# Expert scores of the first two query tiles: whole tiles in three float32r passes instead of exchanged halves in float32

## The chip, the cores and the metric

The kernel runs on one core of a Trainium2 chip. The metric is the device time of one execution in microseconds (us). The time before is 422.52 us, the median of 3 runs (422.43 to 423.71). One more execution was recorded by the hardware profiler; all durations below are from it.

## What is computed

The reference is a sparse attention over 8 batches, 8 heads, 576 positions and head size 64, followed by a mixture of four experts (E = 4), each of which is a causal attention of its own over x, the first attention's output (8 x 576 x 512):

```python
for e in range(E):
    q = x @ wq[e]; k = x @ wk[e]; v = x @ wv[e]          # 576 x 64 each
    scores = scale * (q @ k.transpose(0, 2, 1))
    causal = np.triu(np.ones((S, S), dtype=bool), 1)
    scores = np.where(causal, -1000000000.0, scores)
    scores = scores - scores.max(-1, keepdims=True)
    a = np.exp(scores)
    a /= a.sum(-1, keepdims=True) + 1e-09
    ye = a @ v @ wo[e]
    for kk in range(K):                                   # the two chosen experts
        mask = topk[:, :, kk] == e
        out += mask[..., None] * w[:, :, kk:kk + 1] * ye
```

## The kernel before

Everything is written as small operations (`op`), each with one engine or a choice of two, and the tiles that it reads and writes. A list of numbers, ORDER, fixes the order in which all 2579 operations are issued; SECOND names those that take the second engine of their choice; FILL puts extra matmuls on the identity (L305), whose result nobody reads, ahead of some operations. Each engine works its own instructions strictly in this order.

Stage 1 (`stage1`) makes x: for each batch and each pair of heads it loads q, k and v, turns them, takes local or strided scores, a softmax, and splits x into a high and a low float32r part (`xh`, `xl`). Stage 2 works by batch and by pairs of experts (`ep` is 0 or 1; the two experts of a pair, a = 0 and 1, lie in the lower and upper 64 partitions):

- `project` makes q and k of a pair, 128 partitions by 576 columns, in two cuts of 256 and 320 columns (CUT). Each cut is 12 matmuls (L966; L977 in the first batch), four blocks of x by three products of high and low parts.
- The cuts leave PSUM so: k as float32 (`pj_out`), and from there as a high and a low float32r part (`k_h` L997, `k_l` L1001). Of q the first cut, which serves query tiles 0 and 1, stays float32 (`pj_out`); the second, for tiles 2 and 3, goes straight into high and low parts (`qk_h` L987 on ACT, `qk_l` L989 on DVE), and its last 64 columns also as float32 (`q_out`) for the 64 rows of tile 4.
- `attend` takes scores. Tiles 2 and 3 (`s2`, L1059) go in three passes, high by high, low by high and high by low, 6 matmuls of 384 or 512 columns, float32r, on the array cut as 64 rows by 128 columns. Tiles 0 and 1 (`s2q`, L1047) go in float32 on quarters of 64 by 64, in 8 matmuls: each quarter takes a half tile of 64 queries, and the two halves of tile 0 stand exchanged in PSUM, so that quarters with nearly as many columns run side by side. Such an operation is in the program once per batch and pair, 16 times in all. The recorded float32 matmuls count two to one in the program.
- Since tile 0 is exchanged, it has a mask of its own (`m_sw`, filled by `swapped` on POOL), its gate weights are copied across (`gate_s` into `wts`, 16 small copies), and its output is stored in two halves.
- Tile 4's 64 rows of two pairs are scored by `s2_4` (L1081, float32, quarters), by the cuts of 256 and 320 key columns.
- Then come mask and maximum (`max2`, L1016 on DVE), the exponential (L1021, ACT), the scaling (L1117, POOL), turning (`t2`, L1144), the product with v (`acc`, L1183), and the output projection (`out_tile`, L1217).

A matmul's operands cut the array in different ways (128x128, 64x128, 64x64, 128x64, 32x64, 64x32), and ORDER changes between these cuts 142 times.

Of the kernel before, what the change touches and what calls it, by code (L numbers as in the profile page):

```python
# [22 lines left out]
def attention_moe_kernel(  # L23
# [60 lines left out]
    class Ring:  # L84
# [36 lines left out]
    }  # L121
    ORDER = [
# [136 lines left out]
    ]  # L259
    FILL = {  # L260
        7: 1, 17: 7, 80: 4, 132: 3, 134: 3, 139: 1, 216: 2,
    }

    def op(kind, eng, key, fn, r=(), w=(), mode=None, dmas=(), after=()):
# [70 lines left out]
    def act(n):  # L335
        return 0.06 + 0.00082 * n
# [58 lines left out]
    def swapped(e):  # L395
        nc.gpsimd.memset(m_sw, 0.0)
        keep(m_sw[:64], [[-1, 128]], 64, 1)
        keep(m_sw[64:, :64], [[-1, 64]], 0, 1)
        nc.gpsimd.memset(m_sw[64:, 64:], NONE)
# [895 lines left out]
```

## Time and profile before

| | us |
|---|---|
| median of 3 runs | 422.52 |
| the profiled execution's own time | 422.69 |
| its span, first to last instruction | 421.0 |
| PE (TensorE) busy | 411.0 (98%) |
| DVE (VectorE) busy | 339.8 (81%) |
| ACT (ScalarE) busy | 277.5 (66%) |
| POOL (GpSimd) busy | 230.3 (55%) |

Busy time is the union of an engine's instructions; matmuls overlap each other, so their mean durations are longer than the distance from one to the next. What an operation takes of PE is read here from its start to the start of the next one.

### The profile page before, as it was taken

How to read it: one execution, taken by the hardware profiler on the slowest of the kernel's cores; microseconds unless marked ns; L12 is line 12 of the kernel's file. 1: busy time of each engine (PE TensorE's matmuls, PEld its weight loads, DVE VectorE, ACT ScalarE, POOL GpSimd, SP SyncE). 2: the span in 40 equal slices, each digit the busy share in tenths (PEclk: the TensorE clock that was granted, in tenths of full speed). 3: DMA queues.
4: the chain of work that ended last, by engine and by line, in shares of the span. 5: the costliest groups of instructions: out<-in, count | busy, mean ns of one | idle time of the engine just before them, and what ended most of it. 6: DMA issues, size and time to landing. Idle time of an engine off the chain costs nothing.

```text
span 421.0 us, 18647 instructions
## 1 busy us (share of the span) xinstructions
PE 411.0 (98%) x7523; PEld 358.8 (85%) x7523; DVE 339.8 (81%) x1073; ACT 277.5 (66%) x877; POOL 230.3 (55%) x398
## 2 busy tenths in 40 slices
PE   8889999999999999999999999999999999999996
PEld 5668988987898879998899888998899888997775
DVE  4897898999998899978976699898988896339840
ACT  5677378668776457877767465765666469657862
POOL 5674673776536750699229630589216671185540
PEclk9999999999999999999999999999999999999999
DMA  6667637554656655464356524750443040001033
GB/s 178 194 192 181 121 91 136 100 89 96 112 102 109 146 126 87 94 129 103 72 90 133 134 46 114 129 107 11 114 102 97 20 116 22 2 26 27 27 101 100
DMA packets 156502, 41.86 MB, mean 99 GB/s; under 512 B 146080, under 2 KB 149792, under 8 KB 156416
## 3 DMA queue, kind: packets, MB, share of 16 engines
q1 hardware_dynamic: 156272, 40.54, 43.9%
q8 instruction: 59, 0.97, 1.0%
q14 instruction: 27, 0.22, 0.2%
q10 hardware_dynamic: 144, 0.13, 0.1%
HBM read 31.20 MB, written 9.44 MB: 97 GB/s over the span
## 4 chain that ended last, share of the span: by engine, by line
PE 86%; DVE 5%; ACT 3%; DMA 2%; issue 1%; POOL 1%; SPq 0%; ACTq 0%; POOLq 0%
PE bank L966 22%; PE bank L1217 12%; PE bank L1183 10%; PE bank L895 10%; PE bank L1144 6%; PE bank L1059 5%; PE bank L783 3%; PE bank L802 3%; PE bank L1047 2%; PE bank L689 2%; PE bank L673 2%; PE bank L1081 2%; PE bank L753 2%; PE bank L977 1%; DMA p<-in_q_dram 1%
## 5 line engine op out<-in xcount | busy, mean ns | idle before, releaser
L1021 ACT ACTIVATE p<-p,st 128x384 f32<-128x384 f32 (+3 forms) x128 | 71.5, 561 | 10.8 <-DVE st L1016 10.7
L1117 POOL TENSOR_SCALAR p<-p,st,wt 128x256 f32<-128x256 f32 (+2 forms) x96 | 63.9, 672 | 15.1 <-DVE st L1108 7.4
L1016 DVE CUSTOM_DVE_ANT_0 p<-bank,m_cau 128x384 f32<-128x384 f32 (+2 forms) x96 | 50.0, 548 | 1.2 <-PE bank L1059 0.6
L1183 PE MATMUL bank<-th,vs 128*64 128x192 f32 (+4 forms) x512 | 48.0, 337 | 0.0
L563 DVE STREAM_TRANSPOSE qkt<-nat 128x576 f32<-128x576 f32 x48 | 47.5, 1002 | 0.1
L1183 PEld LDWEIGHTS bank<-th,vs 128*64 128x64 f32 x512 | 33.8, 137 | 13.8 <-issue 7.1
L345 ACT COPY th<-bank 128x256 f32<-128x256 f32 (+2 forms) x108 | 40.4, 434 | 7.6 <-PE bank L1144 7.2
L765 ACT CAST xh<-bank 128x128 fp32r<-128x128 f32 (+4 forms) x112 | 29.4, 320 | 22.3 <-PE bank L783 12.8
L966 PE MATMUL bank<-xh,wh_k 128*128 128x256 f32 (+1 forms) x120 | 36.3, 303 | 0.0
L895 PE MATMUL bank<-wh_v,xh 128*128 128x260 f32 x128 | 36.2, 283 | 0.0
L895 PE MATMUL bank<-wl_v,xh 128*128 128x260 f32 x128 | 36.2, 283 | 0.0
L966 PE MATMUL bank<-xh,wh_q 128*128 128x256 f32 (+1 forms) x120 | 36.1, 301 | 0.1
L767 DVE TENSOR_TENSOR xl<-bank,xh 128x128 fp32r<-128x128 f32 (+4 forms) x112 | 31.8, 322 | 5.3 <-ACT xh L765 5.0
L895 PE MATMUL bank<-wh_v,xl 128*128 128x260 f32 x128 | 35.9, 281 | 0.0
L966 PE MATMUL bank<-xl,wh_k 128*128 128x256 f32 (+1 forms) x120 | 35.5, 296 | 0.0
L966 PE MATMUL bank<-xh,wl_k 128*128 128x256 f32 (+1 forms) x120 | 35.5, 296 | 0.0
L966 PE MATMUL bank<-xl,wh_q 128*128 128x256 f32 (+1 forms) x120 | 35.5, 296 | 0.0
L966 PE MATMUL bank<-xh,wl_q 128*128 128x256 f32 (+1 forms) x120 | 35.5, 296 | 0.0
L1144 PEld LDWEIGHTS bank<-ident,p 64*128 64x128 f32 x800 | 30.2, 139 | 5.7 <-issue 1.3
L716 POOL TENSOR_TENSOR p1l<-p1l,st 128x640 f32<-128x640 f32 (+1 forms) x18 | 20.7, 1151 | 25.7 <-DVE st L714 25.5
L1144 PE MATMUL bank<-ident,p 64*128 64x64 f32 x800 | 33.7, 226 | 0.5 <-DVE p1l L703 0.3
L727 POOL TENSOR_TENSOR p1l<-p1l,st 128x640 f32<-128x640 f32 (+1 forms) x18 | 20.5, 1141 | 18.6 <-DVE st L725 15.2
(190 smaller groups left out, 1220.1 us busy)
## 6 DMA issues: line engine op xcount, KB each, us to landing
nat<-in_q_dram SPq DMA_DIRECT2D x96, 72.0 KB
nat<-in_k_dram SPq DMA_DIRECT2D x96, 72.0 KB
out_dram<-ys SPq DMA_DIRECT2D x23, 256.0 KB
v<-in_v_dram SPq DMA_DIRECT2D x96, 40.0 KB
out_dram<-ys SPq DMA_DIRECT2D x25, 128.0 KB
v<-in_v_dram SPq DMA_DIRECT2D x48, 54.0 KB
v<-in_v_dram SPq DMA_DIRECT2D x32, 48.0 KB
v<-in_v_dram SPq DMA_DIRECT2D x32, 45.0 KB
```

The source lines that it names most:

```text
L345: (nc.scalar.copy if e == "ACT" else nc.vector.tensor_copy)(dst, src)
L563: op("tq", {"DVE": 0.66 if local else 1.11}, k0 - 13, lambda e, x=x: nc.vector.transpose(turned(qkt.t, x), raw(x) if local else raw(x).rea ...
L765: op("xh", {"ACT": act(n_) + 0.04 * (not local)}, key, lambda e, s_=s_, x_=x_: nc.scalar.copy(x_(xh.t), s_(xa.t)), r=[xa], w=[xh[u]])
L767: op("xl", {"DVE": dve(n_)}, key + 0.5, lambda e, s_=s_, x_=x_: nc.vector.tensor_sub(x_(xl.t), s_(xa.t), x_(f(xh.t))), r=[xa, xh[u]], w=[x ...
L895: nc.tensor.matmul(vp.t[:, :NV], xx.t[:, t0:t0 + 128], ww.t[:, kt, :], start=i == 0, stop=i == 11)
L966: nc.tensor.matmul(pj.t[:, :n_], ww.t[:, kt, ep * 128:(ep + 1) * 128], xx.t[:, c], start=i == 0, stop=i == 11)
L1016: op("max2", {"DVE": 0.08 + 0.00104 * nk}, k_ + 0.5, lambda e, a=a: nc.vector.tensor_tensor_reduce(out=p.t[:, a, :nk], in0=sp[a].t[:, so:s ...
L1021: op("exp2", {"ACT": 0.285 + 0.00084 * nk}, k_ + 1, lambda e, a=a: nc.scalar.activation(p.t[:, a, :nk], p.t[:, a, :nk], AF.Exp, bias=st.t[ ...
L1117: lambda e, p=p, a=a, ci=ci, t=t, nk=nk, s_=s_, ep=ep: nc.gpsimd.tensor_scalar(p.t[:, a, :nk], p.t[:, a, :nk], s_.t[:, 20 + ci + a:21 + ci ...
L1144: nc.tensor.transpose(tp[hf].t[:, 64 * c:64 * c + 64], src, ident[r, r])
L1183: nc.tensor.matmul(acc.t[o, c0:c0 + cn], vw, th[ep, a].t[:, s0:s0 + cn], start=j == 0, stop=j == nj - 1, skip_group_check=True)
L1217: nc.tensor.matmul(yp.t[:, :n_], xx.t[:, c0:c0 + 128], ww.t[:, ep, c], start=i == 0, stop=i == 5)
```

## The change

The first cut of q is now split into high and low parts like the second; `qk_h` and `qk_l` are issued for both cuts and the float32 copy of the first cut is gone. The scores of tiles 0 and 1 are whole tiles in three passes: 6 matmuls of 256 columns, then 6 of 128 columns, on the 64x128 cut. With that the mask `m_sw`, the copies `gate_s` and the two-part store of tile 0 are gone; the key columns of `s2_4` are cut as 448 and 128, and its mask `m_last` is 128 columns wide. In the last batch the two stores of tile 4 are operations of their own. ORDER, SECOND and FILL are new throughout.

```diff
     FILL = {
-        7: 1, 17: 7, 80: 4, 132: 3, 134: 3, 139: 1, 216: 2,
+        54: 2, 6: 2,
     }
...
-    LATER += [op("init", {"POOL": 1.5}, 0.0, fn) for fn in (causal, swapped, lasts, lambda e: pads(e, 0), lambda e: pads(e, 1))]
+    LATER += [op("init", {"POOL": 1.5}, 0.0, fn) for fn in (causal, lasts, lambda e: pads(e, 0), lambda e: pads(e, 1))]
...
-    QK2 = ring("qk2", [128, LO + 64 + S], 2)
-    QKR = ring("qkr", [128, 2 * (S - LO) + 2 * S], 2, F32R)
+    QK2 = ring("qk2", [128, 64 + S], 2)
+    QKR = ring("qkr", [128, 4 * S], 2, F32R)
...
-        ws = WS[b] = WTS.new(f"wts_{b}")
-        for i in range(2):
-            s_, o_ = slice(64 * i, 64 * i + 64), slice(64 - 64 * i, 128 - 64 * i)
-            op("gate_s", either(E), key + 4 * step + 0.6, lambda e, wt=WT[b], s_=s_, o_=o_: copy(
-                e, ws.t[o_], wt.t[s_, 0, :E]), r=[WT[b]], w=[ws[i]])
...
-            if u and not j:
+            if not j:
...
-                        def mmq(e, sp=sp, qk=qk):
-                            for c0, nq, x, h in ((0, 64, 1, 0), (0, 128, 0, 1), (128, 256, 1, 1), (128, 192, 0, 0)):
-                                for a in range(2):
-                                    r = slice(64 * a, 64 * a + 64)
-                                    q_ = c0 + 64 * h
-                                    nc.tensor.matmul(sp[a].t[64 * x:64 * x + 64, c0:c0 + nq], qk_lo(qk, 0, q_, 64)[r],
-                                                     qk_lo(qk, 1, 0, nq)[r], start=True, stop=True)
...
+                        def mm2(e, sp=sp, qk=qk):
+                            for c0, n_ in ((128, 256), (0, 128)):
+                                for i, (qq, kk) in enumerate(passes(qk, c0, 128, 0, n_)):
+                                    for a in range(2):
+                                        r = slice(64 * a, 64 * a + 64)
+                                        nc.tensor.matmul(sp[a].t[:, c0:c0 + n_], qq[r], kk[r], start=i == 0, stop=i == 2)
...
-                c0, n_ = CUT[hh]
+                c0, n_ = ((0, S - 128), (S - 128, 128))[hh]
```

The order at the places that matter below. First PE at the program's start, before: after the warm-up matmuls (L355) come transposes of the first pairs of heads (L611, L624) and fillers (L305); eight of the 21 fillers stand here, and the other 13 later in the start.

```order
L611 MATMUL bank_65<-ident,p_162 128x128 x4
L624 MATMUL bank_66<-ident,p_162 128x128 x2
L305 LDWEIGHTS ident
L305 MATMUL bank_67<-ident 128x512
L611 MATMUL bank_67<-ident,p_163 128x128 x4
...
L305 MATMUL bank_68<-ident 128x512
L624 MATMUL bank_68<-ident,p_163 128x128 x2
L611 MATMUL bank_69<-ident,p_163 128x128 x4
```

The same place now (L603 and L616 are the transposes, L304 the fillers, L665 the first local scores):

```order
L603 MATMUL bank_64<-ident,p_161 128x128 x4
L304 LDWEIGHTS ident
L304 MATMUL bank_65<-ident 128x512
...
L616 MATMUL bank_67<-ident,p_162 128x128 x2
L304 LDWEIGHTS ident
L304 MATMUL bank_68<-ident 128x512
...
L603 MATMUL bank_68<-ident,p_161 128x128 x4
L665 MATMUL bank_69<-qkt_171 32x64
```

Four fillers are left, two at each of these places, and none behind them.

Second, PE in one of the later batches, before: `s2q` (L1047) stands between two `s2_4` (L1081), which use the same quarters of the array.

```order
L1081 MATMUL bank_67<-qk_153 64x256
L1047 MATMUL bank_65<-qk_153 64x64
L1047 MATMUL bank_68<-qk_153 64x64
L1047 MATMUL bank_65<-qk_153 64x128
L1047 MATMUL bank_68<-qk_153 64x128
L1047 MATMUL bank_65<-qk_153 64x256
L1047 MATMUL bank_68<-qk_153 64x256
L1047 MATMUL bank_65<-qk_153 64x192
L1047 MATMUL bank_68<-qk_153 64x192
L1081 MATMUL bank_71<-qk_152 64x320
```

Now, near the same place (L1034 is the new operation, L1203 the output projection, L1130 the turning `t2`); the pair of 256 columns and the pair of 128 stand three times each:

```order
L1203 MATMUL bank_66<-wl_o_239,oh_221 128x512
L1034 MATMUL bank_64<-qkr_153 128x256
L1034 MATMUL bank_71<-qkr_153 128x256
...
L1034 MATMUL bank_64<-qkr_153 128x128
L1034 MATMUL bank_71<-qkr_153 128x128
...
L1130 MATMUL bank_68<-ident,p_161 128x64
```

The operation now stands next to `t2` or another `s2`, which use the 64x128 cut too; over the whole program the cut changes 138 times instead of 142.

Third, DVE at the first q and k of the first batch, before: the low part of k's second cut (L1001), the float32 copy of q's first cut (L345), the low part of q's second cut (L989).

```order
L1001 TENSOR_TENSOR qkr_154<-qk_152,qkr_154 128x320
L345 COPY qk_152<-bank_66 128x256
L989 TENSOR_TENSOR qkr_154<-bank_65,qkr_154 128x320
L723 TENSOR_REDUCE st_184<-st_184 128x10
L725 RECIPROCAL st_184<-st_184 128x10
L1001 TENSOR_TENSOR qkr_154<-qk_152,qkr_154 128x256
L1016 ISA p_158,st_218<-bank_67,m_cau 128x256
```

Now (L975 makes the low parts of q, L988 those of k, L344 copies k's first cut, L1003 is `max2`):

```order
L344 COPY qk_151<-bank_69 128x256
L975 TENSOR_TENSOR qkr_153<-bank_64,qkr_153 128x256
L988 TENSOR_TENSOR qkr_153<-qk_151,qkr_153 128x320
L975 TENSOR_TENSOR qkr_153<-bank_66,qkr_153 128x320
L344 COPY qkt_169<-bank_65 128x9x2x18
L695 TENSOR_TENSOR p1s_175<-bank_69,m_str 128x6x54
L1003 ISA p_157,st_215<-bank_70,m_cau 128x256
```

DVE has the low part of both cuts of q, and the first scores wait for it; the low part of k's first cut went to POOL here.

## Rows read from the trace of the kernel before

**Rows 1.** The page: busy time by engine, PE and its clock in 40 slices.

```profile
PE 411.0 (98%) x7523; PEld 358.8 (85%) x7523; DVE 339.8 (81%) x1073; ACT 277.5 (66%) x877; POOL 230.3 (55%) x398
PE   8889999999999999999999999999999999999996
PEclk9999999999999999999999999999999999999999
PE 86%; DVE 5%; ACT 3%; DMA 2%; issue 1%; POOL 1%; SPq 0%; ACTq 0%; POOLq 0%
```

**Rows 2.** Engines by stage: window, its us, busy us of each engine, clock, DMA.

```profile
0.00:46.00 46.00, 41.47 (x939) 32.16 (x940) 35.53 (x113) 30.95 (x86) 27.99 (x74) 1.00 0.71 183
46.00:142.00 96.00, 95.45 (x1873) 85.83 (x1874) 87.75 (x262) 66.27 (x210) 60.56 (x92) 1.00 0.56 106
158.00:266.00 108.00, 107.95 (x2122) 96.84 (x2115) 92.28 (x299) 74.53 (x242) 55.45 (x87) 1.00 0.50 101
376.00:417.00 41.00, 40.90 (x485) 31.96 (x484) 26.68 (x96) 28.33 (x88) 20.37 (x36) 1.00 0.19 58
```

**Rows 3.** PE in order of time around `s2q`: start, us, instructions (two places).

```profile
305.64 0.66 PE L1081 MATMUL bank<-qk 64*64 64x256 f32 x8
306.12 0.73 PE L1047 MATMUL bank<-qk 64*64 64x128 f32 x16
306.66 0.76 PE L1081 MATMUL bank<-qk 64*64 64x320 f32 x8
...
384.28 0.77 PE L1047 MATMUL bank<-qk 64*64 64x64 f32 x16
384.98 1.20 PE L1183 MATMUL bank<-th,vs 128*64 128x192 f32 x12
```

**Rows 4.** PE in order of time around the three-pass scores `s2` (L1059).

```profile
198.69 0.77 PE L1059 MATMUL bank<-qkr 64*128 64x384 f32 x6
199.30 0.66 PE L1144 MATMUL bank<-ident,p 64*128 64x64 f32 x16
199.76 0.94 PE L1059 MATMUL bank<-qkr 64*128 64x512 f32 x6
200.54 0.54 PE L753 MATMUL bank<-ident,p1s 64*128 64x64 f32 x12
...
201.13 1.47 PE L1059 MATMUL bank<-qkr 64*128 64x384 f32 x12
202.43 0.35 PE L1144 MATMUL bank<-ident,p 64*128 64x64 f32 x6
```

**Rows 5.** DVE by line and shape: busy us, mean ns, idle before.

```profile
L989 DVE TENSOR_TENSOR qkr<-bank,qkr 128x320 fp32r<-128x320 f32 x16 | 7.6, 480 | 0.0
L345 DVE COPY qk<-bank 128x256 f32<-128x256 f32 x11 | 4.5, 410 | 4.1 <-PE bank L966 4.0
L345 DVE COPY wts<-wt 64x4 f32<-64x4 f32 x6 | 1.7, 283 | 0.1
```

**Rows 6.** The chain of waits over the start: start, us, what.

```profile
2.18 4.56 DMA p<-in_q_dram
6.74 0.04 issue
6.79 0.78 PE bank L611 x4
7.57 1.51 PE bank L305 x7
...
13.77 0.65 PE bank L305 x3
...
45.77 0.32 PE bank L895
```

**Rows 7.** PE and DVE in order of time in the start.

```profile
1.37 2.74 PE L355 MATMUL bank<-p1l 128*128 128x384 bf16 x8 [1.37 <-DVE p1l L353]
3.91 1.94 PE L611 MATMUL bank<-ident,p 128*128 128x128 f32 x8
...
7.41 1.67 PE L305 MATMUL bank<-ident 128*128 128x512 bf16 x7
8.92 0.38 PE L624 MATMUL bank<-ident,p 128*128 128x128 f32 x2
...
17.61 0.63 PE L611 MATMUL bank<-ident,nat 128*128 128x128 f32 x4
18.08 1.03 PE L305 MATMUL bank<-ident 128*128 128x512 bf16 x4
...
8.42 2.68 DVE L345 COPY qkt<-bank 64x256 f32<-64x256 f32 x6 [1.81 <-ACT qkt L345]
```

More of the change, by code (lines that the diff above doesn't have):

```diff
@@ L367, in attention_moe_kernel @@
     m_cau = const.tile([128, S], F32, name="m_cau")
-    m_last = const.tile([128, S - LO], F32, name="m_last")
-    m_sw = const.tile([128, 128], F32, name="m_sw")
+    m_last = const.tile([128, 128], F32, name="m_last")
     for m in (m_loc, m_str):
@@ L393, in causal @@
         nc.gpsimd.memset(m_cau[:64, S - 64:], NONE)
[L395 to L399, printed above, removed]
     def lasts(e):
@@ L403, in lasts @@
         for hf in range(2):
-            keep(m_last[64 * hf:64 * hf + 64, S - LO - 64:], [[-1, 64]], 0, 1)
+            keep(m_last[64 * hf:64 * hf + 64, 64:], [[-1, 64]], 0, 1)
         nc.gpsimd.memset(tie, 1.0)
@@ L841, in attention_moe_kernel @@
     OF = {}
-    O, VSB, WT, WL, WS = {}, {}, {}, {}, {}
+    O, VSB, WT, WL = {}, {}, {}, {}
     def split3(x, w):
@@ L943, in qk_lo @@
     def qk_lo(t, j, c, n):
[L945 removed]
+        o = 64 + c if j else c - S + 64
         return t.lo.t[:, o:o + n]
     def qk_hl(t, i, j, c, n):
[L950 removed]
+        o = (2 * j + i) * S + c
         return t.hl.t[:, o:o + n]
@@ L985, in project @@
             k_ = key + step * u + 0.5
-            if u and not j:
-                op("qk_h", {"ACT": act(n_)}, k_, lambda e, pj=pj, n_=n_: nc.scalar.copy(
-                    qk_hl(qk, 0, 0, LO, n_), pj.t[:, :n_]), r=[pj], w=[qk[0, 1]])
-                op("qk_l", {"DVE": dve(n_)}, k_ + 0.1, lambda e, pj=pj, n_=n_: nc.vector.tensor_sub(
-                    qk_hl(qk, 1, 0, LO, n_), pj.t[:, :n_], f(qk_hl(qk, 0, 0, LO, n_))), r=[pj, qk[0, 1]], w=[qk[0, 1]])
-                op("q_out", either(64), k_ + 0.2, lambda e, pj=pj, n_=n_: copy(
-                    e, qk_lo(qk, 0, S - 64, 64), pj.t[:, n_ - 64:n_]), r=[pj], w=[qk[0, 2]])
+            if not j:
+                op("qk_h", {"ACT": act(n_)}, k_, lambda e, pj=pj, c0=c0, n_=n_: nc.scalar.copy(
+                    qk_hl(qk, 0, 0, c0, n_), pj.t[:, :n_]), r=[pj], w=[qk[0, u]])
+                op("qk_l", {"DVE": dve(n_)}, k_ + 0.1, lambda e, pj=pj, c0=c0, n_=n_: nc.vector.tensor_sub(
+                    qk_hl(qk, 1, 0, c0, n_), pj.t[:, :n_], f(qk_hl(qk, 0, 0, c0, n_))), r=[pj, qk[0, u]], w=[qk[0, u]])
+                if u:
+                    op("q_out", either(64), k_ + 0.2, lambda e, pj=pj, n_=n_: copy(
+                        e, qk_lo(qk, 0, S - 64, 64), pj.t[:, n_ - 64:n_]), r=[pj], w=[qk[0, 2]])
                 continue
@@ L1007, in attend @@
     def attend(b, qks, un, key):
-        vs, wt, ws = VSB[b], WT[b], WS[b]
+        vs, wt = VSB[b], WT[b]
         p2, st, keys, ends = {}, {}, {}, {}
@@ L1013, in scored @@
         def scored(t, so, nk, p, sp, st, ci, k_):
-            msk = m_cau[:, S - nk:] if t else m_sw
+            msk = m_cau[:, S - nk:]
             for a in range(2):
@@ L1041, in attend @@
                     if t == 1:
-                        def mmq(e, sp=sp, qk=qk):
-                            for c0, nq, x, h in ((0, 64, 1, 0), (0, 128, 0, 1), (128, 256, 1, 1), (128, 192, 0, 0)):
-                                for a in range(2):
-                                    r = slice(64 * a, 64 * a + 64)
-                                    q_ = c0 + 64 * h
-                                    nc.tensor.matmul(sp[a].t[64 * x:64 * x + 64, c0:c0 + nq], qk_lo(qk, 0, q_, 64)[r],
-                                                     qk_lo(qk, 1, 0, nq)[r], start=True, stop=True)
-                        op("s2q", {"PE": 0.58}, k_, mmq, r=[qk[0, 0], qk[1, 0]], w=[*sp, *(p2[ep, i][a] for i in range(2) for a in range(2))], mode=MQ)
+                        def mm2(e, sp=sp, qk=qk):
[4 more added lines that the diff above has]
+                                        nc.tensor.matmul(sp[a].t[:, c0:c0 + n_], qq[r], kk[r], start=i == 0, stop=i == 2)
+                        op("s2", {"PE": 0.69}, k_, mm2, r=[qk[0, 0], qk["h0"]], w=[*sp, *(p2[ep, i][a] for i in range(2) for a in range(2))], mode=MR)
                 else:
@@ L1082, in mml @@
                                              qk_lo(qks[c], 1, c0, n_)[h], start=True, stop=True)
-                op("s2_4", {"PE": 0.53}, k_ + 0.2 * hh, mml, r=[y for x in qks.values() for y in (x[0, 2], x[1, hh])], w=[*sp, *(p[hh] for p in pl)], mode=MQ)
+                op("s2_4", {"PE": 0.53}, k_ + 0.2 * hh, mml, r=[y for x in qks.values() for y in (x[0, 2], *((x[1, 0],) if hh == 0 else ()), x[1, 1])], w=[*sp, *(p[hh] for p in pl)], mode=MQ)
                 for a, p in enumerate(pl):
@@ L1221, in out_tile, with store @@
             op("yp_out", either(n_), key + h + 0.5, lambda e, yp=yp, c=c: copy(e, ys.t[:, c], yp.t[:, :n_]), r=[yp], w=[ys[h]])
-            def store(e, c=c):
-                t0 = QT[t][0]
-                dma = nc.scalar if e == "ACT" else nc.sync
-                if last:
-                    dma.dma_start(out[b - 1, t0:, :], ys.t[:64, :])
-                    dma.dma_start(out[b, t0:, :], ys.t[64:, :])
-                elif t == 0:
-                    dma.dma_start(out[b, 64:128, :], ys.t[:64, :])
-                    dma.dma_start(out[b, :64, :], ys.t[64:, :])
-                else:
-                    dma.dma_start(out[b, t0:t0 + 128, c], ys.t[:, c])
-            op("store", {"SP": 0.5, "ACT": 0.5} if b == B - 1 else {"SP": 0.5}, key + h + 1, store, r=[ys[h]], dmas=[(0.4, 0.4)] * 2 if last or t == 0 else [(0.4, 0.8)])
+            t0 = QT[t][0]
+            end = b == B - 1
+            if last:
+                parts = [(out[b - 1, t0:, :], slice(0, 64)), (out[b, t0:, :], slice(64, 128))]
+            else:
+                parts = [(out[b, t0:t0 + 128, c], slice(0, 128))]
+            def store(e, parts, c=c):
+                for dst, r in parts:
+                    (nc.scalar if e == "ACT" else nc.sync).dma_start(dst, ys.t[r, c])
+            for y, ps in enumerate([[x] for x in parts] if end else [parts]):
+                op("store", {"SP": 0.5, "ACT": 0.5} if end else {"SP": 0.5}, key + h + 1 + 0.1 * y, lambda e, ps=ps, store=store: store(e, ps),
+                   r=[ys[h]], dmas=[(0.4, 0.8 / len(parts))] * len(ps))
     for hp in START:
```

9 lines of the change are left out of this document (3 added, 6 removed), and 295 rows, old and new, of tables (ORDER, SECOND).

## The prediction

> **What bounds the kernel now.** I read the busy times first. PE is busy 411.0 us of a span of 421.0, 98%, DVE 81%, ACT 66%, POOL 55% [rows 1]. In the 40 slices only the first three and the last stand below nine tenths. The table by stage says the same in microseconds: in the first 46 us PE is busy 41.47, and after that 95.45 of 96, 107.95 of 108, 40.90 of 41 [rows 2]. The chain that ended last runs over PE for 86% of the span [rows 1]. So from 46 us on, whatever changes PE's work changes the end by as much, and work of DVE, ACT and POOL costs only if it makes PE wait. The first 46 us are another thing: there the chain goes from a load over transposes and fillers to DVE, ACT and POOL and back [rows 6], and PE waits for its data. A busy PE is not PE at its peak, so for an operation I do not take its busy time, which overlaps its neighbours, but the distance from its start to the start of the next operation.
>
> **What it removes from PE.** 16 operations `s2q`. Between two `s2_4`, on the same cut of the array, one takes from 306.12 to 306.66, 0.54 us [rows 3]. Where a change of the cut follows, it takes from 384.28 to 384.98, 0.70 us [rows 3]. The difference, 0.16 us, I take as the price of one change of the cut, and count these changes apart.
>
> **What it adds to PE.** 16 operations of three passes over 256 columns and three over 128. The trace has no such shape, so I work from `s2`: three passes over 384 columns take from 198.69 to 199.30, 0.61 us; over 512 columns from 199.76 to 200.54, 0.78 us [rows 4]. 128 more columns cost 0.17, and 3 x 128 columns at the level of 2.4 GHz are 0.16, so the columns are paid at full speed. Then three passes over 256 columns alone are 0.61 - 0.17 = 0.44, and over 128 alone 0.44 - 0.17 = 0.27. Two `s2` in a row take from 201.13 to 202.43, 1.30 us, where apart they are 0.61 + 0.78 = 1.39 [rows 4]. The lower bound is 0.61, the 384-column operation, as if only columns counted. The upper bound for the forecast is 0.44 + 0.27 = 0.71, as if the second group began anew. I take 0.66, the middle, since it pays for six more weight loads but not for a new start. The difference to `s2q` is 0.66 - 0.54 = 0.12, times 16 = +1.9 us (bounds 0.07 and 0.17: 1.1 and 2.7). All of it lies on the path, since PE does.
>
> Whether passes over 128 columns hold this pace is the open point. Each of them brings a load of 128 columns of weights for only 128 moving columns. The nearest row is the turning: 16 matmuls of 64 columns, each with a load of that size, take from 199.30 to 199.76, 0.46 us, 29 ns each, or 58 ns for the two that lie in the two halves of the rows [rows 4]; 128 columns need 53 ns, so loads at this pace about keep up. The Trainium skill ("TensorE: Matmul & The Clock Gate", LDWEIGHTS) speaks against the change here: it gives a weight load as its columns divided by 1.2 per ns, some 107 ns for 128. By that the three narrow pairs would take 0.32 us, the operation 0.44 + 0.32 = 0.76, and the sum would be 3.5 us instead of 1.9, by my estimate; the 29 ns of the trace disagree with it.
>
> **Changes of the cut.** The order has 142 before and 138 now. At 0.16 us that is 4 x 0.16 = -0.6 us.
>
> **Other engines.** DVE gets 16 low parts of 256 columns. At 320 columns one takes 480 ns; the copy of 256 columns takes 410 [rows 5], so 16 x 0.41 = 6.6 us. The order takes other things off it: 7 copies out of the projections (2.9 us), all 6 of its `gate_s` copies at 283 ns (1.7 us) [rows 5], and it trades copies of other kinds with ACT. DVE ends some 3 us fuller, under 1% of the span. From 46 to 142 us it is busy 87.75 of 96 [rows 2], so there is room, though little. The cost is between 0 and 3 us; I take +0.4, because PE in the same stretch waited only 0.55 us. The first scores now wait for the split of k and q, but the order has put other work between: of 433 PE operations 79 follow their last producer without another PE operation between in the old order, and 79 in the new. I read from this that the new order is as tight as the old, no more. `m_sw`, `gate_s` on ACT, eight fewer stores' issues on SP and the other cut of `s2_4` (the same columns in all) lie beside PE's work and count nothing; if that cover went, they would be about 0.3 us a copy.
>
> **Fillers.** 17 of 21 go. Seven of them stand in the chain of the start with 1.51 us, three more with 0.65 [rows 6], so at most 2.2 us go. But behind them the chain passes to DVE and ACT, and DVE's first copies, at 8.42, had waited 1.81 us for ACT, not for PE [rows 7]. So most of it should be found again as waiting. Between 0 and -2.2 I take -0.4. That is also my allowance for the new order of the start, which has nearly the same 61 PE operations before the first projection of v as the old.
>
> **The sum.** 1.9 - 0.6 + 0.4 - 0.4 = +1.3 us. The profiled execution took 422.69 us (span 421.0 and 1.7 around it), so the changed kernel takes 424.0 us. Against the median of 422.52, 0.17 lower, that is +0.35%. Its own range is 422.8 (the scores at their lower bound, DVE at nothing: 1.1 - 0.6 - 0.4) to 425.8 (the upper bound, 1 us of DVE, no gain from the fillers: 2.7 - 0.6 + 1.0).
>
> **Rivals.** *The start gives back more than the scores cost.* The fillers leave 2.2 us of the chain of the start, and POOL loses the filling of `m_sw` there. For it: PE is busy only 41.47 of the first 46 us [rows 2], so there is something to win. Against it: the start is carried by loads, DVE, ACT and POOL, whose work before the first projection of v is the same but for two or three operations. With all 2.2 us and the low price of the scores: 422.69 + 1.1 - 0.6 - 2.2 = 421.0. It decides as soon as the first projection of v starts over 1.5 us earlier. Chance 0.25.
>
> *Narrow float32r passes do not run at the columns' pace.* If 128 columns cost as much as 256, the operation is 0.44 + 0.44 = 0.88, 0.34 over `s2q`, 16 x 0.34 = 5.4 us; the total, with the other terms (-0.6 + 0.4 - 0.4) as above, is 427.5. At float32's pace (two transposes of 128 columns from 17.61 to 18.08, 0.235 each [rows 7]) the narrow passes are 0.70, the operation 1.14, 0.60 over `s2q`, and the total 422.69 + 9.6 - 0.6 = 431.7. For it: no float32r matmul of fewer than 256 columns is in this kernel, so nothing shows it. Against it: from 512 to 384 columns the price fell in full. It is the case on the slow side; it decides from 0.75 us per operation on. By the Trainium skill's load time above it would end near 425.6. Chance 0.17.
>
> *The clock falls in the start.* The first eight warm-up matmuls take 2.54 us to the next operation, 318 ns for 384 columns, the 1.2 GHz level; the seven fillers at 7.41 take 1.51, 216 ns for 512 columns, the 2.4 GHz level [rows 7], though the clock row shows full speed throughout [rows 1]. Between the two stood transposes and a filler; the later fillers keep PE at work where it would wait. Without them some of the work between 8 and 28 us could run at half speed. If that hits 5 us of work and waiting hides half, it costs 2.5 us: 426.5. The Trainium skill (same page, Part 1) has the gate closed by default and opened by activity; the trace agrees as far as the slow first eight go. Chance 0.08.
>
> **How the numbers follow.** A measurement of this kernel tells about 0.3% from no change, 1.27 us: below 421.25 is faster, above 423.79 slower. The forecast has 0.50, of which I put 0.33 above 423.79 and 0.17 within. The start rival gives 0.16 faster and 0.09 within; the other two, 0.25, are slower. Faster 0.16, within 0.3% 0.26, slower 0.58. The range reaches from the start rival, a little under its 421.0, to the first of the narrow rival's prices: 420.2 to 428.0; outside I leave about 0.1 at the top and 0.08 at the bottom.
>
> **What the profile will show.** L1034 from start to next start: 0.61 to 0.71 us if I am right, 0.88 or more if narrow passes are dear. PE's matmuls of 128 columns there some 60 ns from pair to pair, not 107 or 230. The first projection of v (L886) near 45.77 us, where it starts now [rows 6]; earlier by 1.5 us or more if the start rival holds. The transposes and scores between 8 and 28 us at the same durations, unless the clock fell. PE's waits after 46 us still around 1.5 us; if they grow by 2 us with DVE as releaser, the order or the fuller DVE was underpriced. A PE that waits for low parts of q (L975) ahead of L1034 would prove me wrong on the added wait.

## The result and the profile after

The changed kernel takes 428.83 us (median of 4 runs, 428.68 to 428.94) against 422.48 before (now the median of 4 runs too): 1.0144 of it, 95% interval 1.0124 to 1.0164. The forecast was 424.0 with a range up to 428.0: right on the side, 4.8 us short. The profiled execution has a span of 427.1 us, 6.1 more than before.

The page after; its lines answer to [rows 1]:

```profile
span 427.1 us, 18469 instructions
PE 410.4 (96%) x7442; PEld 360.6 (84%) x7442; DVE 342.9 (80%) x1069; ACT 277.3 (65%) x878; POOL 231.1 (54%) x397
PEclk9899999999999999999999999999999999999999
PE 81%; DVE 10%; ACT 3%; issue 2%; POOL 2%; DMA 1%; SPq 0%; DVEq 0%; POOLq 0%
```

PE is busy 0.6 us less than before in a span 6.1 longer: the loss is waiting. The stages, as in [rows 2]:

```profile
0.00:46.00 46.00, 38.64 (x908) 31.10 (x912) 34.97 (x110) 30.16 (x83) 28.25 (x73) 0.96 0.70 182
46.00:142.00 96.00, 93.60 (x1832) 84.56 (x1822) 88.82 (x259) 64.80 (x209) 57.51 (x83) 1.00 0.55 104
158.00:266.00 108.00, 107.49 (x2098) 95.82 (x2097) 94.11 (x301) 71.26 (x229) 57.83 (x97) 1.00 0.48 101
376.00:417.00 41.00, 40.67 (x469) 32.88 (x469) 26.69 (x96) 27.82 (x87) 21.33 (x38) 1.00 0.14 46
```

From 46 to 142 us PE misses 2.4 us where it missed 0.55. PE's waits after 46 us (engine, line waited for, releaser: us in all, times, longest):

```profile
PE bank L1045 <- DVE ol L1182: 0.9, 1, 0.9
PE bank L665 <- issue: 0.8, 1, 0.8
PE bank L1130 <- DVE th L344: 0.7, 1, 0.7
PE bank L886 <- issue: 0.6, 1, 0.6
PE bank L1045 <- DVE xl L759: 0.5, 1, 0.5
PE bank L681 <- issue: 0.5, 1, 0.5
```

These six are single events. From the start of one matmul to the start of the next, less the usual step, they are 1.03 us (at 97.87), 0.96 (62.19), 0.83 (298.36), 0.77 (281.52), 0.71 (299.60) and 0.68 (257.83): 5.0 us. The other five rows of the list, not shown, are 0.2 to 0.3 us each and 1.3 us together; the whole list of before has four such rows and 1.0 us. I measure what follows from the start of the first projection of v (45.70 us before, 46.26 after) to the end of the span: 375.3 us before, 380.8 after. So of the 6.1 us the start has 0.6, the six waits have 5.0, and everything else 0.5. Three of the waits have DVE as releaser, three have none.

**The three behind DVE.** DVE and GpSimd in order of time at 97 us (start, us, instruction):

```profile
97.10 0.16 DVE L906 TENSOR_TENSOR gt<-lg 128x16 f32<-128x16 f32 x1
97.19 1.23 DVE L907 TENSOR_TENSOR eq<-lg 128x16 f32<-128x16 f32 x1
98.34 0.14 DVE L908 TENSOR_REDUCE mx<-lg 128x1 f32<-128x4 f32 x1
98.41 0.54 DVE L1182 TENSOR_TENSOR ol<-bank,oh 128x384 fp32r<-128x384 f32 x1
```

```profile
97.10 1.28 POOL L719 TENSOR_TENSOR p1l<-p1l,st 128x640 f32<-128x640 f32 x1
```

L907 compares 16 numbers in each partition; elsewhere it takes 0.16 to 0.17 us. Here it takes 1.23 and ends with GpSimd's L719, and the low part L1182, for which PE waits, stands behind it. At 296.57 L906, here on 64 numbers and elsewhere 0.18 to 0.23 us long where it is not held, takes 2.06 us and ends with two of GpSimd's L988 (296.87 to 298.56); both waits of 298 and 299 us are behind that. Over the whole trace the DVE operations that are long against others of their shape are those with their inputs in SBUF (comparisons, differences, scalar_tensor_tensor, before also two copies), and only while GpSimd works; reductions and whatever reads PSUM keep their time to a quarter or 0.1 us, and the transposes of 576 columns have two times, some 0.75 and 1.25 us, both beside GpSimd and without it. Counting those that take over one and a half times the median of their shape and at least 0.25 us more than it, before has 10 with 6.6 us above the median, after 11 with 8.3: not many more, but three waits of PE now stand behind two of them. The Trainium skill ("SBUF — State Buffer", section "SBUF: two separate sides") says that a DVE operation with two inputs in SBUF and a GpSimd operation that reads SBUF lock each other out of a shared port for whole instructions. The trace agrees, with 1.23 us for 0.16.

**The three without a releaser.** They stand in the middle of an operation. PE at 281 us:

```profile
281.40 0.28 PE L886 MATMUL bank<-wl_v,xh 128*128 128x260 f32 x1
281.52 0.28 PE L886 MATMUL bank<-wh_v,xh 128*128 128x260 f32 x1
282.39 0.39 PE L886 MATMUL bank<-wh_v,xl 128*128 128x260 f32 x1 [0.59 <-issue]
```

The page has a DMA queue of instructions:

```profile
q8 instruction: 59, 0.97, 1.0%
```

That is 59 packets of 16.4 kB for PE's 15,059 records, about one for 255 records. Counted from the first record (matmuls, weight loads and semaphore instructions), PE resumes after these waits at record 2497, 10177 and 10945: each is 193 more than a multiple of 256, and each comes 1.2 to 1.6 us after such a packet has landed. In none of the traces here, this one or those of the experiments, does a record 193 + 256n start less than 1.1 us after its packet, and the packet starts at most some 300 records ahead of it. So I read these waits as waits for the next block of instructions: PE has run through the records ahead of it before the block is there. In the changed kernel the blocks with the least time between packet and start are 10177 (1.24 us), 12225 (1.33, where the list has a wait of 0.2) and 2497 (1.41), and 10945 has 1.55; in the trace of before only one block (1.34 us, record 12225) has under 1.7. I call them block waits below.

### The profile page after: what moved, and what is told of

It is laid out like the page before. It is cut to its first block, busy times and chain, and to the rows that moved or that the text cites. A ratio compares the mean times of both kernels' runs of the same rounds, so it can differ in the third digit from the quotient of the medians.

```text
span 427.1 us, 18469 instructions
## 1 busy us (share of the span) xinstructions
PE 410.4 (96%) x7442; PEld 360.6 (84%) x7442; DVE 342.9 (80%) x1069; ACT 277.3 (65%) x878; POOL 231.1 (54%) x397
## 4 chain that ended last, share of the span: by engine, by line
PE 81%; DVE 10%; ACT 3%; issue 2%; POOL 2%; DMA 1%; SPq 0%; DVEq 0%; POOLq 0%
PE bank L952 18%; PE bank L1203 11%; PE bank L1169 10%; PE bank L886 9%; PE bank L1130 6%; PE bank L1045 5%; PE bank L665 3%; PE bank L794 3%; PE bank L775 3%; PE bank L1034 3%; PE bank L681 2%; PE bank L1067 2%; ACT qkt L344 2%; PE bank L963 2%; PE bank L745 1%
## 5 line engine op out<-in xcount | busy, mean ns | idle before, releaser
L1103 POOL TENSOR_SCALAR p<-p,st,wt 128x256 f32<-128x256 f32 (+3 forms) x128 | 77.8, 620 | 34.9 <-DVE st L1094 26.3
L1008 ACT ACTIVATE p<-p,st 128x256 f32<-128x256 f32 (+3 forms) x128 | 71.9, 565 | 14.6 <-DVE st L1003 14.4
L1003 DVE CUSTOM_DVE_ANT_0 p<-bank,m_cau 128x256 f32<-128x256 f32 (+3 forms) x128 | 56.6, 484 | 4.6 <-PE bank L1034 2.6
L344 ACT COPY th<-bank 128x384 f32<-128x384 f32 (+2 forms) x120 | 46.1, 437 | 11.8 <-PE bank L1130 10.0
L1130 PEld LDWEIGHTS bank<-ident,p 64*128 64x128 f32 x800 | 30.1, 139 | 7.8 <-issue 2.3
L1130 PE MATMUL bank<-ident,p 64*128 64x64 f32 x800 | 34.7, 227 | 1.6 <-DVE th L344 0.7
L952 PE MATMUL bank<-xh,wh_k 128*128 128x320 f32 (+1 forms) x120 | 35.7, 297 | 0.0
L952 PE MATMUL bank<-xl,wh_k 128*128 128x320 f32 (+1 forms) x120 | 35.5, 296 | 0.0
L952 PE MATMUL bank<-xh,wl_k 128*128 128x320 f32 (+1 forms) x120 | 35.5, 296 | 0.0
L708 POOL TENSOR_TENSOR p1s<-p1s,st 128x648 f32<-128x648 f32 (+1 forms) x18 | 20.7, 1156 | 16.2 <-DVE st L706 6.6
L719 POOL TENSOR_TENSOR p1l<-p1l,st 128x640 f32<-128x640 f32 (+1 forms) x18 | 20.7, 1154 | 15.4 <-DVE st L717 14.7
```

What stands on the lines that cost most here:

```text
L344: (nc.scalar.copy if e == "ACT" else nc.vector.tensor_copy)(dst, src)
L952: nc.tensor.matmul(pj.t[:, :n_], ww.t[:, kt, ep * 128:(ep + 1) * 128], xx.t[:, c], start=i == 0, stop=i == 11)
L1003: op("max2", {"DVE": 0.08 + 0.00104 * nk}, k_ + 0.5, lambda e, a=a: nc.vector.tensor_tensor_reduce(out=p.t[:, a, :nk], in0=sp[a].t[:, so:s ...
L1008: op("exp2", {"ACT": 0.285 + 0.00084 * nk}, k_ + 1, lambda e, a=a: nc.scalar.activation(p.t[:, a, :nk], p.t[:, a, :nk], AF.Exp, bias=st.t[ ...
L1103: lambda e, p=p, a=a, ci=ci, t=t, nk=nk, s_=s_, ep=ep: nc.gpsimd.tensor_scalar(p.t[:, a, :nk], p.t[:, a, :nk], s_.t[:, 20 + ci + a:21 + ci ...
L1130: nc.tensor.transpose(tp[hf].t[:, 64 * c:64 * c + 64], src, ident[r, r])
```

## Experiments

Times are medians, with the ratio to the kernel before in brackets; "from v" is the distance from the first projection of v to the end of the span. Line numbers shift by a few where an edit adds or removes lines.

### What the new scores cost PE

**Old scores in the new order, new scores in the old one.** ORDER, SECOND and FILL of one kernel were carried over to the operations of the other, operation by operation; nothing else is edited. Of the first one's table a line, before and now:

```diff
     ORDER = [
-        3, 48, 49, 50, 55, 57, 59, 60, 56, 62, 58, 52, 54, 185, 5, 7, 61, 53, 9, 51, 8, 64, 6, 17, 19, 63, 12, 13,
+        6, 12, 14, 4, 2, 15, 48, 49, 55, 57, 56, 50, 52, 53, 60, 61, 185, 64, 62, 58, 59, 51, 54, 5, 63, 7, 9, 10,
...
```

> The operations of the kernel before (float32 scores on quarters, float32 q, exchanged halves) in the new order: each operation stands where its counterpart stands in the changed kernel. Theory: the 6.3 us lost are about 3 us of dearer scores on PE, 0.6 us of the start and some 3 us of waits that the new order makes whatever the scores are; then this run takes about 426 us. Rival: the order is as good as the old one and the waits come from what the new scores wait for (the split of q and k, 16 more operations on DVE); then it takes 422.5 to 423.5 us, as the kernel before.

> The changed kernel's operations in the old order, an operation put off only as far as its inputs ask. Theory: the old start and the old few waits, plus 16 scores at 0.74 instead of some 0.56 us: 422.5 + 3.0 = 425.5 us. Rival (the new dependencies and the fuller DVE make PE wait in any order): 428 us or more.

The first took 431.93 us (1.0223), the second 442.49 (1.0463): both slower than either kernel. No theory had the first; the second lies in its rival's range (428 or more), but so far above both kernels that the dependencies and DVE alone are not shown as the reason. An order fits the durations of its own operations; carried to others it makes waits (in the second one alone one of 3.4 us for GpSimd). So these two runs can't split off the order as a part of the change.

**Passes that alternate.**

```diff
-for c0, n_ in ((128, 256), (0, 128)):
-    for i, (qq, kk) in enumerate(passes(qk, c0, 128, 0, n_)):
+for i in range(3):
+    for c0, n_ in ((128, 256), (0, 128)):
+        qq, kk = passes(qk, c0, 128, 0, n_)[i]
```

> The changed kernel with the new scores' passes in another order: 256, 128, 256, 128, 256, 128 columns instead of 256 three times and then 128 three times. The same matmuls. Theory: a narrow pair takes 110 ns because the weights of the next pair are still loading; beside a wide pair that load is hidden, the narrow pairs take about 60, the operation falls from 0.74 to 0.64 us and the kernel by 16 x 0.10 = 1.6 us, to 427.2 us. Rival: float32r matmuls of 128 columns run at half the pace by themselves; then the operation stays at 0.74 us and the kernel at 428.8 us.

427.84 us (1.0135). The two accumulations alternate in one bank here, and the scores come out different. PE in order of time:

```profile
109.41 0.88 PE L1035 MATMUL bank<-qkr 64*128 64x256 f32 x12
110.14 0.36 PE L745 MATMUL bank<-ident,p1s 64*128 64x64 f32 x6
```

It takes 0.73 us to the next operation, as at the same place in the changed kernel (its rows stand under the next run). From pair to pair of matmuls (the halves of the rows), in the first of these operations, the changed kernel takes 224, 119, 117 ns for the wide passes and 61, 115, 110 for the narrow. Alternating, it is 224, 61, 170, 59, 170, 59: a narrow pair takes 59 ns when its weights are there already, and the wide one behind it then takes 170. The six add up to 743 ns, against 746. Neither theory had this: the narrow matmul is as fast as I said, but its load takes its time wherever it stands.

**64 columns instead of 128.**

```diff
-for c0, n_ in ((128, 256), (0, 128)):
+for c0, n_ in ((128, 256), (0, 64)):
```

> The changed kernel with 64 moving columns in each of the three narrow passes instead of 128, the loads of 128 columns of weights as before. Left out: half of the first tile's scores. Theory (the loads set the pace of narrow passes): the pairs after the first stay at 105 to 115 ns, L1034 stays at 0.70 to 0.75 us. Rival (narrow float32r columns run at half pace): the pairs fall to about 55 ns and L1034 to 0.58 us or less. The time is not told by either: 428.8 by the loads, 426.2 by the columns, and by the runs so far any shift of this size can move it by 1 to 2 us.

430.37 us (1.0178). PE in order of time, first the changed kernel, then this one:

```profile
109.90 0.89 PE L1034 MATMUL bank<-qkr 64*128 64x256 f32 x12
110.63 0.55 PE L745 MATMUL bank<-ident,p1s 64*128 64x64 f32 x12
```

```profile
109.47 0.85 PE L1034 MATMUL bank<-qkr 64*128 64x256 f32 x12
110.16 0.58 PE L745 MATMUL bank<-ident,p1s 64*128 64x64 f32 x12
```

0.73 us and 0.69. The narrow pairs take 31, 112, 112 ns: halving the columns shortens the first pair only, whose load lies behind a wide one. The loads set the pace. The Trainium skill's 107 ns for 128 columns ("TensorE: Matmul & The Clock Gate", LDWEIGHTS), which I had set aside, is near the 110 that the trace shows for these float32r loads. It is not what the float32 turning takes: there, too, the trace has loads of 128 columns (64x128), and a pair follows the last in some 61 ns. That less work took 1.5 us longer belongs to the next part: in this run DVE's L916 takes 2.17 us, where it takes some 0.17 undisturbed, and PE waits 1.8 us at 345.8.

**The price in the order of before.** The old scores get 178 ns more of columns each.

```diff
-for c0, nq, x, h in ((0, 64, 1, 0), (0, 128, 0, 1), ...
+for c0, nq, x, h in ((128, 107, 1, 1), (128, 107, 0, 0), (0, 64, 1, 0), (0, 128, 0, 1), ...
```

> The kernel before, in its own order, with each of the 16 old scores made longer: both halves of the columns of the array get 107 more float32 columns (written first, then written over), 4 x 107 / 2.4 = 178 ns, about what the new scores cost over the old ones. Nothing else is changed. Theory (each order is tight, but the price of the scores itself passes one to one): 422.5 + 16 x 0.178 = 425.4, within 0.6, near the 425.35 that the changed kernel takes without its three held-up places. Rival (a tuned order is upset by any shift of 2 to 3 us, as the order of the kernel before was with the new operations): 426.5 or more, with DVE operations held up beside GpSimd at new places. Rival (other engines set the pace in the stages after 46 us): under 424.

426.93 us (1.0098), 1.5 above the first theory and in the range of the second, but not for its reason: PE's list of waits has no new wait for DVE. From v it takes 378.9 us, 3.6 more than before: 2.7 of columns (15 of the 16 operations stand there) and one wait of 0.47 at record 10433, which is 40 x 256 + 193. So PE's time passes to the end, and the shift brings a block wait of its own.

**Two narrow passes less.**

```diff
 for i, (qq, kk) in enumerate(passes(qk, c0, 128, 0, n_)):
+    if c0 == 0 and i:
+        continue
```

> The changed kernel with only the first of the three narrow passes (high by high) in each of the 16 new scores: 32 pairs of matmuls of 128 columns less, at 112 ns each 3.6 us of PE. Left out: two of three passes of the first tile's scores. Theory (PE's time passes to the end one to one): 428.8 - 3.6 = 425.2, within 0.6. Rival (the freed time turns into waiting, since DVE and ACT set the pace behind the scores): 427.0 or more.

429.47 us (1.0173, four runs from 428.05 to 432.09), although PE has 3.6 us less to do: the rival's time, but not for its reason. The trace is of the slowest of the four. Its longest waits on PE, and the clock in 40 slices:

```profile
PE bank L775 <- DMA nat<-in_k_dram: 2.0, 1, 2.0
PE bank L775 <- DVE st L715: 1.9, 1, 1.9
PE bank L1047 <- DVE ol L1184: 1.1, 1, 1.1
PE bank L1132 <- DVE th L344: 1.1, 1, 1.1
PEclk9999999999999999899999999999899989999999
```

The first, put down to a DMA, resumes at record 7105 = 27 x 256 + 193. The second is a held-up DVE operation again; DVE, then GpSimd:

```profile
344.15 2.28 DVE L916 SCALAR_TENSOR_TENSOR wt<-sel,wt 128x16 f32<-128x16 f32 x1
```

```profile
344.72 1.29 POOL L708 TENSOR_TENSOR p1s<-p1s,st 128x648 f32<-128x648 f32 x1
345.95 0.46 POOL L984 CAST qkr<-qk 128x320 fp32r<-128x320 f32 x1
```

The waits are not all. The granted clock stands at half (1.2 GHz) from 178.0 to 181.5, 300.9 to 304.3 and 348.7 to 352.1 us, each time just behind one of these waits. With all waits of the list taken off, what follows v is 377.0 us here and 375.5 in the changed kernel: 1.5 more, where 3.4 less was to be expected, since 30 of the 32 pairs left out stand there. These 4.9 us fit the 10.3 us at half clock; no run tests them apart.

### The fillers

```diff
-        54: 2, 6: 2,
+        54: 2, 6: 2, 21: 2, 16: 1, 138: 8, 101: 2, 79: 2, 215: 3,
```

> The changed kernel with 18 fillers back in the start, where PE waits between 8 and 28 us. Theory: the clock, which the trace of the changed kernel shows at half from 16.9 to 20.3 us, stays at full speed; the first projection of v begins up to 1.5 us earlier than 46.3 us, and the kernel takes 427.3 to 428.3 us. Rival: the start is carried by DVE, ACT and POOL; the clock stays up, and the time is 428.8 us all the same, or longer if fillers delay work.

428.25 us (1.0143): the theory's time, but the clock did not stay up, it is at half from 26.4 to 29.9 us instead. The start is 1.0 us shorter (v at 45.25), and the block waits at 62, 257 and 281 us are gone; but L916 is held up, PE waits 1.9 us for it, and another block wait of 0.8 comes at 311.9. Nothing is left of the gain.

```diff
-        7: 1, 17: 7, 80: 4, 132: 3, 134: 3, 139: 1, 216: 2,
+        7: 1, 17: 7,
```

> The kernel before without 13 of its 21 fillers: only the one and the seven that follow its first two marked operations stay. By the prediction's term (fillers cost the chain of the start 0 to 2.2 us, of which 0.4 is given back): 422.1, between 420.3 and 422.5. Rival (fillers cover waits, and without them the granted clock falls in the start): slower than 422.8, with the granted clock under 0.99 between 10 and 30 us.

424.76 us (1.0049), against the forecast's sign. The page's clock row, the same slices as in [rows 1]:

```profile
PEclk9969999999999999999999999999999999999999
```

The clock falls in the third slice, v starts at 46.54 instead of 45.70, and a block wait of 1.1 us comes at record 25 x 256 + 193.

### DVE held up by GpSimd

**Three GpSimd operations cut short.**

```diff
+            short[0] = i in (396, 1972, 2015)
...
+                if short[0]:
+                    P, bc[2] = P[:, :, :, :1], bc[2][:, :, :, :1]
                 nc.gpsimd.tensor_tensor(P, P, bc[2], ALU.mult)
```

> The changed kernel, with three GpSimd operations cut to one column: the last softmax step (L719) that runs at 97.10 us, and the two low parts of k (L988) at 296.87 us. Their results are left out but for one column, nothing else is changed. Theory (DVE operations with both operands in SBUF are held up while GpSimd works, and PE waits behind them at three places): DVE's L907 and L906 there fall from 1.23 and 2.06 us to below 0.3, PE's waits at 97.87, 298.36 and 299.60 (1.03, 0.83, 0.71) go, time 426.2 to 427.0. Rival (the order is tight there for other reasons, the next producer is late): the DVE operations shorten, PE waits on at about the same places, 428.3 or more.

425.35 us (1.0068), 3.5 less than the changed kernel and more than expected. The comparisons, on DVE in order of time:

```profile
96.01 0.18 DVE L912 TENSOR_TENSOR eq<-lg 128x16 f32<-128x16 f32 x1
...
294.37 0.42 DVE L911 TENSOR_TENSOR gt<-vs 128x64 f32<-128x64 f32 x1
```

All three waits are gone, and from v it takes 378.3 us, 2.5 less: the 2.6 of the theory. The other 1.0 us is in the start (v at 45.31), which I can't put down to the edit; in this trace the clock stays full in the start, where the changed kernel's is at half from 16.9 to 20.3 us, but no run shows that as the cause.

**Less work on DVE.**

```diff
-    qk_hl(qk, 1, 0, c0, n_), pj.t[:, :n_], ...
+    qk_hl(qk, 1, 0, c0, n_) if u else qk_hl(qk, 1, 0, c0, 1), pj.t[:, :n_ if u else 1], ...
```

> The changed kernel, with the low part of q's first cut (L975, 16 operations of 256 columns on DVE) cut to one column; the pass that would read it reads the high part instead, so PE's work is the same. DVE has some 6 us less to do. Rival (DVE is now too full): PE waits less after 46 us all along, 426.5 or less. Theory (single collisions and the order, not DVE's total): the waits at 97.87, 298.36 and 299.60 stay, 428.0 to 429.3.

427.45 us (1.0119), between the two. The three waits stay as they are (0.9, 0.7, 0.5 in the list of waits). From v it is 379.9, 0.9 less than in the changed kernel. So DVE's fullness costs at most some 1 us.

**Comparisons moved, nothing left out.** In ORDER `gate14` (1270) and `gate1` (2002) go further back, in the first try behind 13 and 17 operations of DVE, in the second behind one and six (its lines are shown):

```diff
-        366, 368, 373, 369, 367, 548, 1270, 1218, 1219, 1220, 1245, 1246, 484, 1240, 1242, 1309, 1243, 1244, 1247,
+        1304, 199, 386, 387, 512, 514, 513, 515, 372, 1268, 366, 368, 373, 369, 367, 548, 1218, 1219, 1220, 1270,
...
-        2122, 965, 991, 992, 2002, 920, 921, 2115, 2117, 2123, 993, 2127, 2116, 882, 922, 962, 963, 1953, 2106,
+        2127, 2116, 882, 922, 962, 963, 1953, 2106, 2118, 2120, 1959, 923, 2119, 1961, 1960, 1956, 1958, 2002, 2128,
```

> The changed kernel with nothing left out: two entries of its order are moved, so that on DVE the gate comparisons (L906, L907) that were held up at 97.19 and 296.57 us stand behind the low parts and copies that PE waits for (the first behind 13 other DVE operations, the second behind 17), still ahead of the GpSimd step that reads them. Theory (PE waits behind DVE operations that GpSimd holds up): wherever they are held now, PE's waits at 97.87, 298.36 and 299.60 (2.6 us together) go, 425.5 to 427.0. Rival (it is GpSimd's load, not DVE's queue, that PE waits for there): PE's waits stay at these places, 428.3 or more. Rival (a shift of 2 us puts other operations beside GpSimd's): the three waits go, others of 1 us and more come elsewhere, 427.5 or more.

> The changed kernel with nothing left out: the gate comparisons of DVE that were held up at 97.19 and 296.57 us stand behind one low part (L1182) and behind six copies, low parts and reductions that PE needs first. Theory (held-up DVE operations ahead of what PE needs): PE's waits at 97.87, 298.36 and 299.60 fall from 2.6 us to under 1, and GpSimd's wait for the comparisons stays under 2 us: 426.0 to 427.3. Rival (the waits move on, as with the far move): 428.3 or more.

The far move took 429.64 us (1.0176). The three waits went, but GpSimd, which reads the comparisons and has a softmax step queued behind, now waited for DVE, and PE behind that:

```profile
304.82 0.22 POOL L909 TENSOR_TENSOR wt<-vs,mx 128x16 f32<-128x16 f32 x1 [6.86 <-DVE mx L906]
```

```profile
PE bank L773 <- DVE st L1001: 1.8, 1, 1.8
```

The near move took 428.06 (1.0129). Its waits:

```profile
PE bank L884 <- issue: 1.1, 1, 1.1
PE bank L679 <- issue: 1.0, 1, 1.0
PE bank L663 <- DVE qkt L553: 0.7, 1, 0.7
PE bank L1032 <- issue: 0.6, 1, 0.6
PE bank L663 <- issue: 0.5, 1, 0.5
```

The held-up comparisons no longer count, except that a transpose is late at 97.85. In their place PE waits 3.2 us without a releaser, four times, where by the same view it waited 1.9 three times. Why these grew I can't say.

### The ends of the instruction blocks

**Two fillers more**, that is four records.

```diff
-        54: 2, 6: 2,
+        54: 3, 6: 3,
```

> The changed kernel with two fillers more in the start, that is four PE instructions more ahead of everything after 10 us. Theory (the waits in the middle of an operation at 62.19, 257.83 and 281.52, 0.96, 0.68 and 0.77 us, without a releaser, are waits for the next block of instructions): they stand between the instructions that lie exactly four earlier in the program. Rival (they belong to the operations): they stand between the same instructions as before. Rival (chance): at other places or gone. Time 428.3 to 429.3 in all three.

428.25 us (1.0138). The wait at 62 us is gone (the block of record 2497 starts 2.8 us after its packet here), the two others resume at record 10177 and 10945 again, which now hold what stood four records earlier in the program. PE at 281 us; the wait stands two matmuls earlier in the projection than above:

```profile
281.07 0.28 PE L886 MATMUL bank<-wh_v,xh 128*128 128x260 f32 x1
281.19 0.28 PE L886 MATMUL bank<-wh_v,xl 128*128 128x260 f32 x1
282.28 0.39 PE L886 MATMUL bank<-wl_v,xh 128*128 128x260 f32 x1 [0.81 <-issue]
```

The theory holds. In the traces of all these kernels together, the lists have 33 waits without a releaser of 0.3 us or more after 46 us, and all 33 end at a record 193 + 256n; the trace of before has none.

**Both causes at once**: the near move and 18 fillers more.

> The same with 18 fillers more in the start, which shift every later PE instruction by 36 against the blocks of 256. Theory (the waits without a releaser in the middle of operations belong to the blocks): those at 257.8 and 281.5 us (0.68, 0.77) go, others may come where a block now ends in a stretch of short matmuls; the time within 1.5 us of that without the fillers, and a granted clock in the start that differs costs nothing. Rival (they belong to the order): they stay at the same operations.

423.40 us (10 runs, nine from 422.43 to 424.50 and one of 430.03), 1.0017 of before, 1.0005 to 1.0029. No block wait is left after 46 us. Its waits and stages:

```profile
PE bank L663 <- DVE qkt L553: 0.7, 1, 0.7
PE bank L1128 <- DVE xl L757: 0.3, 1, 0.3
PE bank L1128 <- DVE ys L342: 0.3, 1, 0.3
```

```profile
46.00:142.00 96.00, 94.62 (x1863) 85.75 (x1860) 89.77 (x263) 65.44 (x211) 59.08 (x86) 1.00 0.54 104
158.00:266.00 108.00, 108.00 (x2085) 96.70 (x2074) 94.44 (x303) 71.86 (x234) 58.62 (x98) 1.00 0.49 102
```

The time fell by 4.7 us and not within 1.5 as I had written, since the block waits had grown to 3.2 us. From v it is 375.7 us, 0.4 more than before: with both causes all but gone, the changed kernel is all but as fast as the old one. The start is long here (v at 46.92), with a block wait of 1.3 us at 24.3.

**Two more**: the comparison of 97 us behind the transpose as well, and then three fillers more.

> The changed kernel with the gate comparison of 296 us moved as in the last two, the one of 97 us behind a transpose of DVE (L553) as well, and the 18 fillers more. Theory (DVE's queue ahead of what PE waits for): the wait of 0.70 us at 97.85 goes, 422.4 to 423.2. Rival (any such move shifts waits elsewhere): 423.5 or more.

> The same with three fillers more in the start (25 in all), six instructions more ahead of everything after 20 us. Theory (block ends in dense stretches of matmuls cost about 1 us each): waits without a releaser stand only at instruction 193 modulo 256 of PE's stream, at places six instructions earlier in the program; the time differs by 0 to 1.5 us either way. Rival (blocks have nothing to do with it): such waits stay at the same operations as in the run without the three fillers.

424.10 us (1.0025, 1.0013 to 1.0037), which is the rival's time, and 426.45 (1.0082), 2.4 more and so outside the 0 to 1.5 of the theory. In the first the wait for the transpose went and a block wait of 0.7 came at 309.4 (record 12225 = 47 x 256 + 193): no gain. In the second, block waits stand at 961 and 7361, both 193 modulo 256, and L914, the operation called L916 above, is held up for 2.28 us once more, which costs PE 1.9, and behind that wait the clock is at half from 344.0 to 347.4 us. No version was faster than before.

## Why the prediction was wrong

**The scores.** The bounds of 0.61 to 0.71 us for an operation failed: where the cut stays, it takes 0.72 to 0.75. I had taken the load's price from the turning in float32 [rows 4] and set the Trainium skill's 107 ns ("TensorE: Matmul & The Clock Gate", LDWEIGHTS) aside for it. The turning loads 128 columns too, but in float32; loads in float32r take nearly twice its 58 ns, and I carried the price across. I gave this case 0.17 and a threshold of 0.75 us; the operation stays just below it. The term itself came out near its 1.9 us by luck, since the other side was wrong as well: 0.54 us is near the lowest price of the old operations, not the usual one. Added up from each start to the next matmul's, over the 15 that follow the first projection of v, the old operations take 9.6 us, 0.64 each, and the new ones 11.1, 0.74 each, in the run with both causes at once. That is 1.5 us more for all 16.

**Changes of the cut and other PE work.** The -0.6 is not measured by itself. With the idle time of the lists of waits taken off, what follows v takes 374.3 us before and 373.9 in the run with both causes at once, so PE's work as a whole did not grow by the 1.9 - 0.6 that I had added up. Two neighbours on the same cut became cheaper by the same sums, the turning (29.7 to 28.8) and the other three-pass scores (21.5 to 21.0); whether the cut is the reason is not shown.

**"The new order is as tight as the old."** This is the step that failed and made the miss. I had counted how many PE operations follow their last producer directly, 79 and 79, and put +0.4 (0 to 3) on everything between the engines. The six new waits were 5.0 us. The count saw the sequence, not the durations: comparisons of some 0.2 us that become 1.23 and 2.06 beside GpSimd, and blocks of instructions that end in a dense stretch of short matmuls. Both can be seen in the trace of before only as events that do no harm (DVE's 10 held-up operations; no block wait in PE's list), so the old order looked looser than it was. That PE's waits would grow with DVE as releaser was written as the sign of a wrong price; that half of them would have no releaser was not foreseen.

**DVE.** +3 us of work, as computed (339.8 to 342.9). As a load it costs at most some 1 us, as the run with less work on DVE shows; it costs through two operations that GpSimd holds up, with three waits of PE behind them.

**Fillers and the start.** Forecast -0.4, measured +0.6 (v at 46.26). The clock did fall, its second slice stands at 8, which I had as a rival at 0.08 and 2.5 us; but the changed kernel with 18 fillers put back, v a microsecond earlier, ends only 0.6 us sooner, and one run of the changed kernel at clock 1.000 took 428.94. Without 13 of its fillers the kernel before is 2.1 us slower. So fillers are worth something by what they cover and by where they put the block ends, and the term had the wrong sign.

**What held.** The side, but by luck: I had forecast it from PE's added work, of which nothing is left in the sum from v on, and it came from waits. PE as the engine that bounds; no wait for low parts of q ahead of L1034; the narrow matmuls themselves at 59 ns a pair.

## What to carry to other kernels

In a kernel that is tuned until one engine is 98% busy, price the waits that a new order can make, not only the work that it moves: a range upward of several microseconds is right even where the work nearly cancels. Look in the trace for short operations of an engine that now and then take several times as long, see what runs beside them, and keep what the bounding engine waits for ahead of them in the queue. Where waits have no releaser, count the instructions: if they stand a whole number of blocks apart, a few idle instructions more or fewer move them.

## What the hardware showed that I had not expected

- A DVE operation on 16 numbers per partition in SBUF takes up to 2.28 us beside GpSimd, across two GpSimd operations in a row, where it takes some 0.17 otherwise.
- PE waits up to 2.0 us where a block of 256 instructions ends (there the list names a DMA; 1.1 where it names no releaser), and goes on 1.2 to 1.6 us after the packet of the next has landed. The Trainium skill ("Runtime: NRT & Kernel Launch", section "Instruction fetch mechanics") has the blocks of 256 and calls their cost mostly hidden; the blocks are as it says, the cost is not.
- Weight loads of 128 float32r columns pass at some 110 ns for the two halves of the rows together, whether 64 or 128 columns move; loads of 128 columns in float32, for the turning, pass at some 61.
- Behind waits of 0.9 to 3.4 us the granted clock fell to half (1.2 GHz) in some traces, three times in that with two narrow passes less, but not behind every such wait: one of 1.8 us in the run with 64 columns left it full.
